# Pooled attention and two MoE layers: a different weight conversion, q transposed on TensorE, half of the k/v pooling in the DMA

## The chip, the cores and the metric

The kernel runs on one core of a Trainium2 chip. The metric is device time in microseconds (us), shorter is better. The engines are called PE (TensorE matmul), PEld (its weight loads), DVE (VectorE), ACT (ScalarE), POOL (GpSimd) and SP (SyncE, which here issues DMAs).

## What is computed

Three parts in float32, one after the other. Weights arrive as 64-bit floats.

```python
# q, k, v: (8 batches, 8 heads, 576, 64)
k_p = k.reshape(B, H, 72, 8, D).mean(axis=3)      # v_p likewise
scores = (1 / sqrt(D)) * q @ k_p.T
attn = exp(scores - max); attn /= attn.sum() + 1e-9
x = (attn @ v_p), as (4608 tokens, 512)
x = ((x @ w1) * (x @ w2)) @ w3 @ w_out            # d_ff 1024
xn = x / sqrt(mean(x * x) + 1e-6) * rms_g
out = (silu(xn @ w_gate) * (xn @ w_val)) @ w_out2 # d_ff 1536
```

## The kernel before, in words

**Numbers.** Every wide product runs as three float32r matmuls (`mm3`, L87 to L90): each operand is split into hi and lo (`split`, L83: ACT copies hi, DVE subtracts), and hi*hi, hi*lo and lo*hi accumulate in PSUM. (a*b) @ w3 @ w_out is computed as (a*b) @ (w3 @ w_out).

**Weights.** `Conv` (L96) turns 64-bit floats into float32. Step s0 loads 128 x 512 words of 64 bits into a tile raw. Step s1: ACT scales the low word (L115); DVE takes the sign out of the high word (L116) and masks the sign off its top 16 bits (L119); ACT subtracts 14336 from those 16 bits and clips at zero (L122, the rebias of the exponent). Step s2: DVE shifts the high word by 3 and ors the sign in (L125) and adds the low part (L133). Step s3 splits. `conv_steps` staggers the steps of successive jobs. There are 76 jobs: 24 for w3 and w_out and 16 for w1 and w2 early on, 12 for the second w_out and 24 for w_gate and w_val later. Tiles raw have 5 buffers for the first 24 jobs and 3 for the rest; the k/v loads share those 3.

**Stages.** Phase 0 forms w3 @ w_out (16 stages of four transposes and four float32 matmuls), with the attention of batch 0, the first half of w1 and w2 and the first products beside it. Phase 1 goes through nine blocks of 512 tokens. Per block there are eight steps m: two wide products (12 matmuls each; the second is multiplied into the first by DVE, L627, giving f, which is split into hh and hl), then the second product (12 matmuls) of the step before. Beside the products of block i runs the attention of batch i + 1. Phase 2 is the gated layer over nine blocks, without attention.

**Attention of a batch** (`att_steps`, L216). k and v are pooled from raw buffers by `pool_pair` (L197): two heads a load, 72 partitions, three halving adds on DVE (L205 twice, L209). kp is transposed on PE and copied to kT by ACT (L247, L248). q is transposed (`step_Q`, L250): for batches 0 and 1 on PE with ACT copies (L271, L276), for the others in 32 x 32 blocks on DVE (L265), 40 instructions a batch. Per tile of 128 rows, five a batch, and per half of the heads: score matmuls (L289), maximum on DVE (L301), its scaling (L302), four exponentials on ACT (L305). Then the normalization (`step_N`, L314): for batches 0 and 1 one DVE multiplication (L324), else eight ACT scalings (L322). Then the transposes to aT (`step_T`, L331), for batches from 2 on by DVE (L339, 54 a batch). `av_step` (L387) multiplies aT with vp and writes xh (ACT, L402) and xl (DVE, L403), the input of a block.

**What sets the order.** `Ticker` spreads these steps over a block's 24 slots, three a step m; `att_of(i)` (L630) lists them, and the block finishes them within 3 * 8 - 1 = 23 slots (L691). A scheduler then orders each engine's instructions; on the chip every engine runs its queue in that order, and an instruction that waits holds up those behind it. SP issues the DMAs in its own order too. PSUM has four buffers ps, used by products, scores, transposes and attention-value matmuls alike, and four for y. At a block's end `y_end` (L580) squares and copies y, sends it to DRAM and forms row sums; POOL computes their power -0.5 (L609).

Of the kernel before, what the change touches and what calls it, by code (L numbers as in the profile page):

```python
# [8 lines left out]
F32 = mybir.dt.float32  # L9
# [3 lines left out]
U16 = mybir.dt.uint16  # L13
# [8 lines left out]
def kernel(  # L22
# [15 lines left out]
    # Float32 products run as three float32r passes: every operand is split  # L38
    # exactly into hi (12 significant bits) + lo (the remaining 12), and
    # hi*hi + hi*lo + lo*hi accumulate in PSUM.  # L40
    # (a*b) @ w3 @ w_out is computed as (a*b) @ (w3 @ w_out).
# [50 lines left out]
    # float64 words -> float32 bits, round to nearest even.  The weights come in  # L92
    # as 64-bit words; the exponent is rebased (14336 = (1023 - 127) << 4, with
    # values below float32's range going to zero), the top 20 mantissa bits are
    # shifted into place and the next 32 bits are rounded to the last 3.
    class Conv:  # L96
# [11 lines left out]
        def s1(self):  # L108
# [3 lines left out]
            top = self.raw.bitcast(U16).rearrange("p (n w) -> p n w", w=4)[:, :, 3]  # L112
            if self.out is None:
# [3 lines left out]
                out=self.out, in0=self.hiw, scalar1=-(2**31), scalar2=None, op0=ALU.bitwise_and  # L117
            )
            nc.vector.tensor_scalar(  # L119
                out=top, in0=top, scalar1=0x7FFF, scalar2=None, op0=ALU.bitwise_and  # L120
            )
            nc.scalar.activation(top, top, AF.Relu, bias=nbias)  # L122

        def s2(self):
            nc.vector.scalar_tensor_tensor(  # L125
                out=self.out,
                in0=self.hiw,
                scalar=3,
                in1=self.out,
                op0=ALU.logical_shift_left,  # L130
                op1=ALU.bitwise_or,
            )
            nc.vector.tensor_tensor(out=self.out, in0=self.out, in1=self.low, op=ALU.add)  # L133
# [29 lines left out]
    nbias = const.tile([P, 1], F32, name="nbias")  # L163
    nc.vector.memset(nbias, -14336.0)
# [32 lines left out]
    def pool_pair(dst, src, b, p):  # L197
        r = raw_p.tile([P, 1024], I32, tag="raw", name="kv")[:SP].bitcast(F32)
        r = r.rearrange("s (h c) -> s h c", h=2)
        nc.sync.dma_start(  # L200
            out=r, in_=src[b, 2 * p : 2 * p + 2].rearrange("h (s l) d -> s h (l d)", l=POOL)
        )
        n = POOL * D // 2
        while n > D:
            nc.vector.tensor_tensor(  # L205
                out=r[:, :, :n], in0=r[:, :, :n], in1=r[:, :, n : 2 * n], op=ALU.add
            )
            n //= 2
        nc.vector.tensor_tensor(  # L209
            out=dst.rearrange("s (h d) -> s h d", d=D)[:, 2 * p : 2 * p + 2, :],  # L210
# [5 lines left out]
    def att_steps(b):  # L216
        q_t, qT_t, s_t, mx_t, den_t = {}, {}, {}, {}, {}
# [10 lines left out]
        def step_k0():  # L228
            st8["kp", b] = at_p.tile([SP, H * D], F32, tag="kp", name="kp")
            for p in range(2):  # L230
                pool_pair(st8["kp", b], k, b, p)

        def step_k1():
            load_q(0)
            for p in range(2, NP):
                pool_pair(st8["kp", b], k, b, p)
            load_q(1)

        def step_kT():
# [7 lines left out]
            nc.scalar.copy(kT[:D, :, :SP], pv[:D])  # L247
            nc.scalar.copy(kT[D:, :, SP:], pv[D:])  # L248

        def step_Q(g, hf):  # L250
# [8 lines left out]
            if b >= 2:  # L259
                src = qt.rearrange("s u (p c) -> s u p c", p=NP)  # L260
                for i in range(2 * hf, min(2 * hf + 2, n // 32)):
                    rows = slice(32 * i, 32 * i + 32)
                    for j in range(4):
                        cols = slice(32 * j, 32 * j + 32)
                        nc.vector.transpose(  # L265
                            qT[cols, :nu, :, rows], src[rows, :nu, :, cols]
                        )
            elif hf < nu:
# [14 lines left out]
        def step_S(t, hf):  # L283
# [17 lines left out]
            nc.vector.tensor_reduce(out=mx, in_=pv, axis=AX.X, op=ALU.max)  # L301
            nc.vector.tensor_scalar_mul(mx, mx, -ATT_SCALE)  # L302
            for j in range(4):
# [6 lines left out]
                    scale=ATT_SCALE,  # L310
# [3 lines left out]
        def step_N(t):  # L314
# [4 lines left out]
            if b >= 2:  # L319
                for h in range(H):  # L320
                    z = s_t[t][:n, h, :SP]
                    nc.scalar.activation(z, z, AF.Copy, scale=den[:n, h, :])  # L322
                return
# [29 lines left out]
        def step_v(ps_):  # L353
            if ps_[0] == 0:
                st8["vp", b] = at_p.tile([SP, H * D], F32, tag="vp", name="vp")
            for p in ps_:
                pool_pair(st8["vp", b], v, b, p)
# [24 lines left out]
        steps[5:5] = [lambda: step_v((0, 1))]  # L382
        steps[11:11] = [lambda: step_v((2, 3))]
# [255 lines left out]
    class Pipe:  # L639
        """The two wide products of m, then the second product of m - 1."""  # L640
# [49 lines left out]
    for i in range(1, NB - 2):  # L690
        pipe.run(i, range(KF1), ab, y_mm, Ticker(att_of(i), 3 * KF1 - 1))  # L691
        xt.pop(i)
# [150 lines left out]
```

## Time and profile before

| | |
|---|---|
| time, median of 3 runs | 1769.09 us (1768.5 to 1769.53) |
| span of the profiled execution, its own time | 1769.0 us |
| PE busy | 1691.3 us, 96% |
| DVE busy | 1011.3 us, 57% |
| ACT busy | 680.2 us, 38% |
| POOL busy | 11.4 us, 1% |
| DMA | 100.17 MB, mean 57 GB/s |

The span runs from the first to the last instruction of one profiled execution; nothing of that execution's time lies outside it that the profile shows. Busy is the union of an engine's instructions. Matmuls overlap in the pipeline and their ends are modelled, so PE's busy time says little of how close it is to its peak; the number of matmuls in a stretch says more. PEclk is the TensorE clock that was granted, 1.00 being 2.4 GHz and 0.50 being 1.2 GHz. A wait is put down to what came last by the profile.

### The profile page before, as it was taken

What the parts mean: (1) busy time and instruction counts of PE and PEld (TensorE: products, weight loads), DVE (VectorE), ACT (ScalarE), POOL (GpSimd) and SP (SyncE); (2) the same over time, 40 slices, a digit from 0 to 9 for tenths busy, and PEclk for the clock granted to TensorE, in tenths of its full rate; (3) what the DMA queues carried; (4) which work ended last, traced back from release to release, by engine and by line L of the source; (5) the groups of instructions that cost most, each with busy time, mean ns of one, the idle gap of its engine ahead of it and who ended that gap; (6) DMA issues with size and microseconds to landing.
All of it is one profiled execution on the core that took longest, in us unless ns stands there. A gap on an engine that the chain in (4) does not pass through costs nothing.

```text
span 1769.0 us, 19994 instructions
## 1 busy us (share of the span) xinstructions
PE 1691.3 (96%) x7418; PEld 1323.9 (75%) x7418; DVE 1011.3 (57%) x2060; ACT 680.2 (38%) x1706; POOL 11.4 (1%) x17
## 2 busy tenths in 40 slices
PE   6989998989898989899999999999999999999999
PEld 3557676767676767678777888888888888888887
DVE  8988898878797967664895232323223232323222
ACT  8977454535353535553783121212111111212111
POOL 0000000000000000000000000000000000000000
PEclk9999999989999989999999999999999999999999
DMA  7745213021212120231452000100000000000000
GB/s 238 200 126 138 75 37 86 20 78 27 79 26 73 32 70 1 72 96 45 133 149 67 31 24 24 30 25 30 23 8 24 30 24 24 19 24 7 24 1 24
DMA packets 84371, 100.17 MB, mean 57 GB/s; under 512 B 44201, under 2 KB 52393, under 8 KB 84274
## 3 DMA queue, kind: packets, MB, share of 16 engines
q1 hardware_dynamic: 84274, 98.90, 19.2%
q8 instruction: 58, 0.95, 0.2%
q14 instruction: 39, 0.32, 0.1%
HBM read 79.97 MB, written 18.91 MB: 56 GB/s over the span
## 4 chain that ended last, share of the span: by engine, by line
PE 64%; DVE 23%; ACT 8%; DMA 3%; issue 2%; SPq 0%; ACTq 0%; DVEq 0%
PE ps L88 14%; PE ps L89 14%; PE ps L90 13%; DVE aT L339 7%; PE y L88 7%; PE y L90 7%; PE y L89 7%; DVE qT L265 3%; ACT raw L122 3%; DVE hl L85 2%; PE ps L395 2%; DVE raw L119 1%; DVE f L627 1%; DVE kv L205 1%; ACT s L322 1%
## 5 line engine op out<-in xcount | busy, mean ns | idle before, releaser
L772 DVE TENSOR_TENSOR f<-ps,f 128x512 f32<-128x512 f32 x108 | 74.7, 691 | 370.1 <-ACT f L771 369.9
L84 ACT CAST hh<-f 128x512 fp32r<-128x512 f32 x185 | 114.7, 620 | 356.3 <-DVE f L775 269.3
L771 ACT ACTIVATE f<-ps 128x512 f32<-128x512 f32 x108 | 64.7, 599 | 384.2 <-PE ps L90 384.0
L85 DVE TENSOR_TENSOR hl<-f,hh 128x512 fp32r<-128x512 f32 x185 | 127.9, 692 | 85.3 <-ACT hh L84 83.6
L88 PE MATMUL y<-o2h,hh 128*128 128x512 f32 x432 | 170.8, 395 | 1.5 <-ACT hh L84 1.5
L90 PE MATMUL y<-o2h,hl 128*128 128x512 f32 x432 | 171.0, 396 | 0.0
L89 PE MATMUL y<-o2l,hh 128*128 128x512 f32 x432 | 170.6, 395 | 0.0
L90 PE MATMUL ps<-xnh,vl 128*128 128x512 f32 x432 | 168.2, 389 | 2.0 <-DVE vl L85 2.0
L89 PE MATMUL ps<-xnl,gh 128*128 128x512 f32 x432 | 169.0, 391 | 0.6 <-DVE xnl L738 0.5
L88 PE MATMUL ps<-xnh,gh 128*128 128x512 f32 x432 | 168.5, 390 | 0.6 <-ACT xnh L737 0.6
L88 PE MATMUL ps<-xnh,vh 128*128 128x512 f32 x432 | 168.6, 390 | 0.5 <-ACT vh L84 0.5
L90 PE MATMUL ps<-xnh,gl 128*128 128x512 f32 x432 | 168.5, 390 | 0.0
L89 PE MATMUL ps<-xnl,vh 128*128 128x512 f32 x432 | 168.3, 390 | 0.0
L339 DVE STREAM_TRANSPOSE aT<-s 32x256 f32<-32x256 f32 x324 | 140.9, 435 | 21.4 <-ACT s L322 15.7
L775 DVE TENSOR_TENSOR f<-ps,f 128x512 f32<-128x512 f32 x108 | 74.7, 691 | 131.2 <-PE ps L90 131.1
L88 PE MATMUL ps<-xh,w2h 128*128 128x512 f32 x288 | 122.3, 425 | 24.4 <-DVE xl L403 19.9
L305 ACT ACTIVATE s<-ps,mx 128x72 f32<-128x72 f32 (+1 forms) x320 | 98.0, 322 | 80.9 <-DVE mx L302 80.8
L88 PE MATMUL y<-hh,wph 128*128 128x512 f32 x288 | 118.6, 412 | 8.9 <-DVE wpl L85 4.5
L88 PE MATMUL ps<-xh,w1h 128*128 128x512 f32 x288 | 118.1, 410 | 2.6 <-ACT s L305 1.3
L122 ACT ACTIVATE raw<-raw,nbias 128x512 uint16<-128x512 uint16 x76 | 110.4, 1460 | 25.6 <-DVE raw L119 25.2
L89 PE MATMUL ps<-xl,w2h 128*128 128x512 f32 x288 | 118.6, 412 | 0.0
L90 PE MATMUL ps<-xh,w2l 128*128 128x512 f32 x288 | 117.9, 409 | 0.0
(110 smaller groups left out, 3061.6 us busy)
## 6 DMA issues: line engine op xcount, KB each, us to landing
raw<-in_moe_w_dram SPq DMA_DIRECT2D x32, 512.0 KB
raw<-in_moe_w_out_dram SPq DMA_DIRECT2D x20, 512.0 KB
kv<-in_k_dram SPq DMA_DIRECT2D x32, 288.0 KB
kv<-in_v_dram SPq DMA_DIRECT2D x32, 288.0 KB
ydram<-f SPq DMA_DIRECT2D x36, 256.0 KB
raw<-ydram SPq DMA_DIRECT2D x18, 512.0 KB
out_dram<-f SPq DMA_DIRECT2D x36, 256.0 KB
q<-in_q_dram SPq DMA_DIRECT2D x32, 256.0 KB
```

The source lines that it names most:

```text
L84: nc.scalar.copy(hi, src)
L85: nc.vector.tensor_tensor(out=lo, in0=src, in1=hi.bitcast(F32), op=ALU.subtract)
L88: nc.tensor.matmul(o, lh, rh, start=first, stop=False)
L89: nc.tensor.matmul(o, lh, rl, start=False, stop=False)
L90: nc.tensor.matmul(o, ll, rh, start=False, stop=last)
L122: nc.scalar.activation(top, top, AF.Relu, bias=nbias)
L265: nc.vector.transpose(qT[cols, :nu, :, rows], src[rows, :nu, :, cols])
L305: nc.scalar.activation(s_t[t][:n, h, :SP], pv[:, j, :], AF.Exp, bias=mx[:, j, :], scale=ATT_SCALE, accum_out=den_t[t][:n, h, :],)
L339: nc.vector.transpose(aT[32 * kb : 32 * kb + 32, :, s0 + 32 * i : s0 + 32 * i + 32], s_t[t][32 * i : 32 * i + 32, :, 32 * kb : 32 * kb + 32],)
L771: nc.scalar.activation(sg, ps, AF.Sigmoid)
L772: nc.vector.tensor_tensor(out=sg, in0=ps, in1=sg, op=ALU.mult)
L775: nc.vector.tensor_tensor(out=hf, in0=ps, in1=a0.pop((i, m)), op=ALU.mult)
```

## The change

1. Conversion: instead of the masking of 16-bit words and ACT's rebias, DVE multiplies the high word, read as a float32, by 2**-112 (which takes 896 off the exponent), and shifts the result by 3 (L117, L120 of the new kernel). The sign is ored into the low part. ACT keeps one operation a job, DVE four.
2. Pooling: a load takes four heads, but only the first four of each eight rows; a second DMA, issued by POOL, adds the other four rows onto them in place (`accum_op=ALU.add`). DVE then adds twice instead of three times, for half as many loads. Loads and sums are separate steps now: k's loads in step_k0, its sums in step_k1; v's loads after the fourth step, its sums seven steps later.
3. The score scale is applied in the copy to kT; the maximum is taken with its sign reversed, so its scaling (L302) goes.
4. q is transposed on PE, with ACT copies, for all batches; the normalization is the one DVE multiplication for all batches. The aT transposes stay as they are.
5. In blocks 1 to 6 the attention steps are spread over 3 * 8 - 4 = 20 slots.

```diff
@@ -109,25 +110,24 @@
             w2_ = self.raw.rearrange("p (n w) -> p n w", w=2)
             self.hiw, self.low = w2_[:, :, 1], w2_[:, :, 0]
             low_u = self.raw.bitcast(U32).rearrange("p (n w) -> p n w", w=2)[:, :, 0]
-            top = self.raw.bitcast(U16).rearrange("p (n w) -> p n w", w=4)[:, :, 3]
+            hi_f = self.raw.bitcast(F32).rearrange("p (n w) -> p n w", w=2)[:, :, 1]
             if self.out is None:
                 self.out = ftile(I32)
             nc.scalar.activation(self.low, low_u, AF.Copy, scale=2.0**-29)
             nc.vector.tensor_scalar(
-                out=self.out, in0=self.hiw, scalar1=-(2**31), scalar2=None, op0=ALU.bitwise_and
+                out=self.out.bitcast(F32), in0=hi_f, scalar1=2.0**-112, scalar2=None, op0=ALU.mult
             )
             nc.vector.tensor_scalar(
-                out=top, in0=top, scalar1=0x7FFF, scalar2=None, op0=ALU.bitwise_and
-            )
-            nc.scalar.activation(top, top, AF.Relu, bias=nbias)
+                out=self.out, in0=self.out, scalar1=3, scalar2=None, op0=ALU.logical_shift_left
+            )
         def s2(self):
             nc.vector.scalar_tensor_tensor(
-                out=self.out,
+                out=self.low,
                 in0=self.hiw,
-                scalar=3,
-                in1=self.out,
-                op0=ALU.logical_shift_left,
+                scalar=-(2**31),
+                in1=self.low,
+                op0=ALU.bitwise_and,
                 op1=ALU.bitwise_or,
             )
             nc.vector.tensor_tensor(out=self.out, in0=self.out, in1=self.low, op=ALU.add)
@@ -194,27 +192,28 @@
     pools[0] = x0_p
     st8 = {}
-    def pool_pair(dst, src, b, p):
+    def pool_four(src, b, g):
         r = raw_p.tile([P, 1024], I32, tag="raw", name="kv")[:SP].bitcast(F32)
-        r = r.rearrange("s (h c) -> s h c", h=2)
-        nc.sync.dma_start(
-            out=r, in_=src[b, 2 * p : 2 * p + 2].rearrange("h (s l) d -> s h (l d)", l=POOL)
+        r = r.rearrange("s (h c) -> s h c", h=4)
+        n = POOL * D // 2
+        w = src[b, 4 * g : 4 * g + 4].rearrange("h (s l) d -> s h (l d)", l=POOL)
+        nc.sync.dma_start(out=r, in_=w[:, :, :n])
+        nc.gpsimd.dma_start(out=r, in_=w[:, :, n:], accum_op=ALU.add)
+        return r
+    def pool_sum(dst, r, g):
+        nc.vector.tensor_tensor(
+            out=r[:, :, : 2 * D], in0=r[:, :, : 2 * D], in1=r[:, :, 2 * D :], op=ALU.add
         )
-        n = POOL * D // 2
-        while n > D:
-            nc.vector.tensor_tensor(
-                out=r[:, :, :n], in0=r[:, :, :n], in1=r[:, :, n : 2 * n], op=ALU.add
-            )
-            n //= 2
         nc.vector.tensor_tensor(
-            out=dst.rearrange("s (h d) -> s h d", d=D)[:, 2 * p : 2 * p + 2, :],
+            out=dst.rearrange("s (h d) -> s h d", d=D)[:, 4 * g : 4 * g + 4, :],
             in0=r[:, :, :D],
             in1=r[:, :, D : 2 * D],
             op=ALU.add,
         )
     def att_steps(b):
-        q_t, qT_t, s_t, mx_t, den_t = {}, {}, {}, {}, {}
+        q_t, qT_t, s_t, mx_t, den_t, kv_t = {}, {}, {}, {}, {}, {}
         def load_q(g):
             if 2 * g >= NTL:
@@ -226,14 +225,13 @@
                 )
         def step_k0():
-            st8["kp", b] = at_p.tile([SP, H * D], F32, tag="kp", name="kp")
-            for p in range(2):
-                pool_pair(st8["kp", b], k, b, p)
+            kv_t["k"] = [pool_four(k, b, g) for g in range(2)]
         def step_k1():
             load_q(0)
-            for p in range(2, NP):
-                pool_pair(st8["kp", b], k, b, p)
+            st8["kp", b] = at_p.tile([SP, H * D], F32, tag="kp", name="kp")
+            for g, r in enumerate(kv_t.pop("k")):
+                pool_sum(st8["kp", b], r, g)
             load_q(1)
         def step_kT():
@@ -244,8 +242,8 @@
                     ps[:, p * SP : (p + 1) * SP], kp[:, p * P : (p + 1) * P], ident[:SP, :SP]
                 )
             pv = ps[:, : NP * SP].rearrange("d (p s) -> d p s", p=NP)
-            nc.scalar.copy(kT[:D, :, :SP], pv[:D])
-            nc.scalar.copy(kT[D:, :, SP:], pv[D:])
+            nc.scalar.activation(kT[:D, :, :SP], pv[:D], AF.Copy, scale=ATT_SCALE)
+            nc.scalar.activation(kT[D:, :, SP:], pv[D:], AF.Copy, scale=ATT_SCALE)
         def step_Q(g, hf):
             if 2 * g >= NTL:
@@ -256,16 +254,7 @@
             if hf == 0:
                 qT_t[g] = at_p.tile([P, 2, NP, P], F32, tag="qT", name="qT", bufs=2)
             qT = qT_t[g]
-            if b >= 2:
-                src = qt.rearrange("s u (p c) -> s u p c", p=NP)
-                for i in range(2 * hf, min(2 * hf + 2, n // 32)):
-                    rows = slice(32 * i, 32 * i + 32)
-                    for j in range(4):
-                        cols = slice(32 * j, 32 * j + 32)
-                        nc.vector.transpose(
-                            qT[cols, :nu, :, rows], src[rows, :nu, :, cols]
-                        )
-            elif hf < nu:
+            if hf < nu:
                 ps = psum()
                 for p in range(NP):
                     nc.tensor.transpose(
@@ -298,8 +287,7 @@
                 mx_t[t] = at_p.tile([P, H, 1], F32, tag="mx", name="mx", bufs=2)
                 den_t[t] = at_p.tile([P, H, 1], F32, tag="den", name="den", bufs=2)
             mx = mx_t[t][:n, 4 * hf : 4 * hf + 4, :]
-            nc.vector.tensor_reduce(out=mx, in_=pv, axis=AX.X, op=ALU.max)
-            nc.vector.tensor_scalar_mul(mx, mx, -ATT_SCALE)
+            nc.vector.tensor_reduce(out=mx, in_=pv, axis=AX.X, op=ALU.max, negate=True)
             for j in range(4):
                 h = 4 * hf + j
                 nc.scalar.activation(
@@ -307,7 +295,6 @@
                     pv[:, j, :],
                     AF.Exp,
                     bias=mx[:, j, :],
-                    scale=ATT_SCALE,
                     accum_out=den_t[t][:n, h, :],
                 )
@@ -316,11 +303,6 @@
             den = den_t.pop(t)
             nc.vector.tensor_scalar_add(den[:n], den[:n], 1e-9)
             nc.vector.reciprocal(out=den[:n], in_=den[:n])
-            if b >= 2:
-                for h in range(H):
-                    z = s_t[t][:n, h, :SP]
-                    nc.scalar.activation(z, z, AF.Copy, scale=den[:n, h, :])
-                return
             nc.vector.tensor_tensor(
                 out=s_t[t][:n, :, :SP],
                 in0=s_t[t][:n, :, :SP],
@@ -350,11 +332,13 @@
             dst = aT[:SP, 4 * hf : 4 * hf + 4, s0 : s0 + n]
             nc.scalar.copy(dst, src)
-        def step_v(ps_):
-            if ps_[0] == 0:
-                st8["vp", b] = at_p.tile([SP, H * D], F32, tag="vp", name="vp")
-            for p in ps_:
-                pool_pair(st8["vp", b], v, b, p)
+        def load_v():
+            kv_t["v"] = [pool_four(v, b, g) for g in range(2)]
+        def step_v():
+            st8["vp", b] = at_p.tile([SP, H * D], F32, tag="vp", name="vp")
+            for g, r in enumerate(kv_t.pop("v")):
+                pool_sum(st8["vp", b], r, g)
         pre = [step_k0, step_k1]
         steps = [step_kT, lambda: step_Q(0, 0), lambda: step_Q(0, 1)]
@@ -379,8 +363,8 @@
                     step_T(t - 1, 1)
             steps += [a, bq, c, d, e]
-        steps[5:5] = [lambda: step_v((0, 1))]
-        steps[11:11] = [lambda: step_v((2, 3))]
+        steps[4:4] = [load_v]
+        steps[11:11] = [step_v]
         steps += [lambda: step_T(NTL - 1, 0), lambda: step_T(NTL - 1, 1)]
         return pre, steps
@@ -688,7 +672,7 @@
     xt.pop(0)
     for i in range(1, NB - 2):
-        pipe.run(i, range(KF1), ab, y_mm, Ticker(att_of(i), 3 * KF1 - 1))
+        pipe.run(i, range(KF1), ab, y_mm, Ticker(att_of(i), 3 * KF1 - 4))
         xt.pop(i)
     for st in att_of(NB - 2):
```

On DVE, at the end of block 1 before (xl_1721 belongs to block 2, of which 384 columns are the newly attended batch; xl_2478 is block 3's; f is a step's product, hl its low part):

```order
L403 SCALAR_TENSOR_TENSOR xl_1721<-ps,xh_1720 128x384
L265 STREAM_TRANSPOSE qT<-q 32x8x32 x9
L403 SCALAR_TENSOR_TENSOR xl_1721<-ps,xh_1720 128x384
L265 STREAM_TRANSPOSE qT<-q 32x8x32
L403 SCALAR_TENSOR_TENSOR xl_1721<-ps,xh_1720 128x384
L265 STREAM_TRANSPOSE qT<-q 32x8x32 x3
L627 TENSOR_TENSOR f<-ps,f 128x512
L403 SCALAR_TENSOR_TENSOR xl_1721<-ps,xh_1720 128x384
L85 TENSOR_TENSOR hl<-f,hh 128x512
L403 SCALAR_TENSOR_TENSOR xl_2478<-ps,xh_2477 128x192 x2
L627 TENSOR_TENSOR f<-ps,f 128x512
L403 SCALAR_TENSOR_TENSOR xl_2478<-ps,xh_2477 128x192
```

The same place now (xl_1609 is block 2's, xl_2291 block 3's, L611 is f, L84 hl):

```order
L387 SCALAR_TENSOR_TENSOR xl_1609<-ps,xh_1608 128x384 x2
L611 TENSOR_TENSOR f<-ps,f 128x512
L387 SCALAR_TENSOR_TENSOR xl_1609<-ps,xh_1608 128x384
L84 TENSOR_TENSOR hl<-f,hh 128x512
L387 SCALAR_TENSOR_TENSOR xl_1609<-ps,xh_1608 128x384
L611 TENSOR_TENSOR f<-ps,f 128x512
L84 TENSOR_TENSOR hl<-f,hh 128x512
L387 SCALAR_TENSOR_TENSOR xl_2291<-ps,xh_2290 128x192 x3
L611 TENSOR_TENSOR f<-ps,f 128x512
```

Block 2's xl moved ahead by one step m (there is an f and an hl between them and block 3's xl), and no qT transposes stand among them.

On DVE right behind that, now, around the start of the next block (vp and kp are the pooled v and k, L208 their last add, which frees a buffer kv; L205 is the first add of a freshly loaded kv; L574 and L577 are y_end's):

```order
L208 TENSOR_TENSOR vp<-kv 72x256
L387 SCALAR_TENSOR_TENSOR xl_2291<-ps,xh_2290 128x192
L208 TENSOR_TENSOR vp<-kv 72x256
L84 TENSOR_TENSOR hl<-f,hh 128x512
L208 TENSOR_TENSOR kp<-kv 72x256
L574 COPY f<-y 128x512
L577 TENSOR_TENSOR f<-f 128x512
L574 COPY f<-y 128x512
L577 TENSOR_TENSOR f<-f 128x512 x2
L205 TENSOR_TENSOR kv<-kv 72x4x128
L84 TENSOR_TENSOR hl<-f,hh 128x512
L208 TENSOR_TENSOR kp<-kv 72x256
```

The first add of the second k load comes nine instructions after the sum that frees a buffer for that load.

On POOL, now, over a block (L201 are the adding DMAs, L593 the power for ss):

```order
L201 DMA kv<-in_k_dram 72x4x256
L201 DMA kv<-in_v_dram 72x4x256 x2
L201 DMA kv<-in_k_dram 72x4x256
L593 TENSOR_TENSOR ss<-ss,mhalf 128x4
L201 DMA kv<-in_k_dram 72x4x256
```

POOL had only the nine L609 there before; four DMAs a batch have come in between them.

## Rows read from the trace of the kernel before

**Rows 1.** The page's first part: busy us, share of the span, xinstructions of each engine.
```profile
PE 1691.3 (96%) x7418; PEld 1323.9 (75%) x7418; DVE 1011.3 (57%) x2060; ACT 680.2 (38%) x1706; POOL 11.4 (1%) x17
```

**Rows 2.** Stages (us): length, busy us (xinstructions) of each engine, granted PEclk, DMA share, GB/s.
```profile
0.00:46.00 46.00, 31.73 (x88) 14.97 (x88) 37.70 (x75) 36.75 (x43) 1.11 (x8) 1.00 0.78 239
46.00:187.00 141.00, 129.44 (x600) 89.22 (x599) 123.73 (x277) 109.21 (x284) 0.00 (x0) 0.99 0.53 144
187.00:709.90 522.90, 486.92 (x2207) 372.17 (x2206) 429.72 (x1048) 245.41 (x938) 6.93 (x6) 0.95 0.19 51
709.90:950.00 240.10, 228.03 (x970) 179.97 (x970) 168.95 (x293) 141.14 (x200) 3.36 (x3) 0.98 0.34 101
950.00:1769.00 819.00, 815.18 (x3559) 667.54 (x3557) 251.16 (x371) 147.69 (x243) 0.00 (x0) 1.00 0.06 22
370.30:380.00 9.70, 9.70 (x48) 7.03 (x48) 2.85 (x6) 2.10 (x5) 0.00 (x0) 1.00 0.26 56
386.00:420.00 34.00, 34.00 (x163) 28.21 (x163) 29.41 (x77) 17.48 (x74) 1.16 (x1) 1.00 0.35 90
1100.00:1200.00 100.00, 100.00 (x438) 81.94 (x437) 31.74 (x47) 18.64 (x31) 0.00 (x0) 1.00 0.07 24
```

**Rows 3.** Groups on PE by shape: first 386 to 420 us, then 370.3 to 380 us.
```profile
L289 PE MATMUL ps<-kT,qT 128*128 128x144 f32 x28 | 4.6, 285 | 0.0
...
L395 PE MATMUL ps<-aT,vp 72*64 72x256 f32 x12 | 1.7, 396 | 0.0
```

**Rows 4.** Waits from 273.4 to 709.9 us: us in total, times, longest us.
```profile
PE ps L88 <- DVE xl L403: 17.1, 5, 3.7
...
PE ps L395 <- DVE f L627: 7.4, 5, 2.2
...
PE ps L88 <- ACT s L305: 5.4, 5, 1.9
```

**Rows 5.** The chain of waits through 355 to 372 us, its shares by line.
```profile
by line: DVE qT L265 22.0%; DVE aT L339 13.0%; PE ps L88 12.2%; PE ps L89 10.0%; PE ps L90 10.0%; PE ps L395 6.2%; issue 5.5%; PE y L88 5.3%; PE y L90 4.1%; DVE f L627 4.1%; DVE hl L85 4.1%; PE y L89 4.0%; DVE xl L403 3.0%
```

**Rows 6.** Groups on DVE in one block, 360 to 448.6 us: xcount | busy us, mean ns | idle before.
```profile
L339 DVE STREAM_TRANSPOSE aT<-s 32x256 f32<-32x256 f32 x54 | 23.5, 435 | 2.9 <-ACT s L322 1.9
L265 DVE STREAM_TRANSPOSE qT<-q 32x256 f32<-32x256 f32 (+1 forms) x40 | 16.4, 409 | 0.7
L205 DVE TENSOR_TENSOR kv<-kv 72x512 f32<-72x512 f32 (+1 forms) x16 | 8.6, 547 | 3.3 <-DMA kv<-in_k_dram 2.2 <-DMA kv<-in_v_dram 1.1
L85 DVE TENSOR_TENSOR hl<-f,hh 128x512 fp32r<-128x512 f32 x9 | 6.2, 689 | 0.9 <-ACT hh L84 0.8
...
L209 DVE TENSOR_TENSOR kp<-kv 72x128 f32<-72x128 f32 x4 | 1.1, 286 | 0.0
```

**Rows 7.** Groups by shape over the whole span.
```profile
L122 ACT ACTIVATE raw<-raw,nbias 128x512 uint16<-128x512 uint16 x76 | 110.4, 1460 | 25.6 <-DVE raw L119 25.2
...
L119 DVE TENSOR_SCALAR raw<-raw 128x512 uint16<-128x512 uint16 x76 | 56.5, 746 | 0.3
...
L133 DVE CUSTOM_DVE_ANT_0 f<-raw,f 128x1024 uint16<-128x1024 uint16 x68 | 47.5, 699 | 0.2
...
L116 DVE TENSOR_SCALAR f<-raw 128x512 int32<-128x512 int32 x68 | 28.6, 421 | 6.2 <-DMA raw<-in_moe_w_dram 4.5 <-DMA raw<-in_moe_w_out_dram 1.0 <-DMA raw<-in_moe_w_val_dram 0.7
...
L324 DVE TENSOR_TENSOR s<-s,den 128x576 f32<-128x576 f32 x8 | 6.0, 748 | 0.0
...
L271 PE MATMUL ps<-ident,q 128*128 128x128 f32 x32 | 4.9, 274 | 0.0
```

**Rows 8.** The whole chain in order of time: start us, us, what.
```profile
386.81 5.50 DMA kv<-in_k_dram
...
570.25 3.20 DMA kv<-in_k_dram
```

More of the change, by code (lines that the diff above doesn't have):

```diff
@@ L12 @@
 U32 = mybir.dt.uint32
-U16 = mybir.dt.uint16
 AF = mybir.ActivationFunctionType
@@ L162 @@
     nc.vector.memset(mhalf, -0.5)
-    nbias = const.tile([P, 1], F32, name="nbias")
-    nc.vector.memset(nbias, -14336.0)
     ydram = dram_p.tile([NB, KD, P, TB], F32, name="ydram")
```

## The prediction

> **What bounds the kernel now.** I read the page first, then the busy time by stage, then inside one block, and last the chain of waits. On the page TensorE (PE) is busy 96% of the span, VectorE (DVE) 57%, ScalarE (ACT) 38% [rows 1]. The stages show what that mean hides: from 950 us to the end PE is busy 815 of 819 us at the full clock, the 2.4 GHz level, VectorE 251, and the change touches nothing there; before 950 VectorE is busy 70 to 88% and ACT 47 to 80% of each stage [rows 2]. Everything is decided before 950.
>
> Blocks 1 to 6 of phase 1 (187 to 709.9 us, one batch of attention beside each block's products) take 522.9/6 = 87.15 us each. What would PE alone need? Between 1100 and 1200 us 438 wide matmuls take 100 us, 0.228 us each; from 386 to 420 us there are 163, 28 of them score matmuls, so (34 - 135 x 0.228)/28 = 0.114 us a score matmul; from 370.3 to 380 us 48, 12 of them attention-value matmuls of 256 columns, so (9.7 - 36 x 0.228)/12 = 0.123 us [rows 2, 3]. A block has 288 wide ones (65.8), 40 score (4.6), 32 attention-value of 288 columns on average (32 x 0.123 x 288/256 = 4.4), four small transposes and two rms matmuls (about 1): 75.7 us. **So 11.4 us of each block are lost.** The waits say where: in the five blocks from 273.4 to 709.9 us PE stood 17.1 us for VectorE's xl and 7.4 us for its product f, once a block each, at the border between two blocks, and 5.4 us for ACT's exponentials in mid-block [rows 4]. That is 30/5 = 6.0 us idle a block. The granted clock of the stage is 0.95 [rows 2]; 0.05 x 87 is 4.4 us more, a tenth of the time at the 1.2 GHz level. Together 10.4, close to 11.4.
>
> What makes the border late? The chain through 355 to 372 us is VectorE first: 22.0% qT transposes (L265), 13.0% aT transposes (L339), 3.0% xl [rows 5]. PE doesn't wait for a long operation but for a queue: qT transposes stand ahead of the xl that free its PSUM buffers.
>
> **The change, part by part.** *In blocks 1 to 6.* VectorE loses per block 40 qT transposes (16.4 us). Of the k/v sums, 8.6 us for the two halvings, 1.1 for kp's last step and as much for vp's, 10.8 in all, there remain four adds of 512 and four of 256 elements, by the same mean of 547 ns 4.4 us [rows 6]. It gains five normalizations at 748 ns, 3.7 us, which leave ACT [rows 7]. Net 16.4 + 6.4 - 3.7 = 19.1 us less, of 429.7/6 = 71.6 [rows 2]: 52.5 us in a block of some 80. (The ten small scalings of mx go too; I don't price them.) PE gains 20 q transposes; between a score matmul's 0.114 us and 4.9/32 = 0.153 us [rows 7] that is 2.3 to 3.1, and I take 2.5, nearer to the first because a row's busy time counts overlapping ends. New floor 78.2 us. The scale of the scores moves into kT's copy, the same two instructions: nothing.
>
> The 20 slots matter as much. In the order rows the xl of a block's own batch stood directly ahead of the next batch's; now a whole product f with its hl stands between, so they are asked for one step m, 36 wide matmuls or 8.2 us, earlier. The border wait was 24.5/5 = 4.9 us, behind 16.4 us of work that will not be in the queue. I count the border as gone, its half clock with it. The price of the 20 slots is density: scores, exponentials and most aT transposes of a batch now lie within about four steps m, where PE needs 4 x 8.2 us and some 6 of attention, 38 us. Outside it VectorE has thirteen operations at 0.69 (four f, four hl, five of y_end), eight xl at less than that and the last ten aT transposes at 0.435 [rows 6]: about 9 + 5 + 4.4 = 18, so 34 us of its 52.5 lie inside. Nearly full; so I keep the mid-block wait (5.4/5 us, its clock about as much again) and add a half for late kv sums: residual 3.0. **81.2 us a block, gain 5.95 x 6 = 35.7 us.**
>
> *The accumulating DMA* is the unknown; no row shows one. A buffer that VectorE's vp sum frees is filled by a plain DMA, then POOL waits for that landing and issues the accumulate, and VectorE's next kv sum waits for the second landing, in its fixed place. The plain half costs 3.2 to 5.5 us by the chain's pieces for kv loads of the same 288 KB [rows 8]. From below I price the second half at the same, 6.4 together; as the upper end I keep four times the slower piece, 22 us, since a read-add-write could be far slower; and I take 11, twice the slower piece. Its cover: the sum stands behind y_end's five operations, which need another 12 matmuls (2.7 us) and cost 5 x 0.69 themselves, about 7 us in all with the hl ahead. So VectorE may stand some 4 us a block, at its start, where the next m's f isn't due for a further 4. POOL's only other work, the pow for ss, stands ahead of the k load in the order rows.
>
> The Trainium skill (DMA: Bandwidth & Descriptors, "Anatomy of one DMA — SWDGE (gpsimd) path") gives a DMA from GpSimd about 2.0 us plus its bytes at 436 GB/s; by that the accumulate would take an estimated 2.7 us, no kv sum would wait, and with a residual of 2.5 the time would be 1707. No row here shows such a DMA, so the sum stays with the bounds above.
>
> *The conversion* (76 of them). ACT loses L122, 1460 ns each, 110.4 us in all. On VectorE a masking of 746 ns (L119) gives way to a shift; its nearest row is the other one-source operation on 128x512 words, 421 ns (L116), which I take, with 421 and 746 as bounds: up to 0.325 us less each, 2.24 instead of 2.56 with the two unchanged ones of 0.70 [rows 7]. From 0 to 46 us the first 16 conversions set the pace, 46/16 = 2.9 us each, though VectorE is busy only 37.7 us; L122 stands in each chain between two of its operations. Without it VectorE paces; its durations overlap a little (37.7 us now for 16 x 2.56 = 41), so about 2.0 us. That could save 13 us; but 512 KB every 2.0 us is 262 GB/s, and 239 GB/s take 0.78 of the DMA engines [rows 2], so I take 9. From 46 to 187 us PE is idle 11.6 us and the clock costs 0.01 x 141 = 1.4, with ACT at 77%: 8 us. From 709.9 to 950 us, 36 conversions beside the products, 12.1 us are idle and 0.02 x 240 = 4.8 go with the clock; ACT drops by 52.6 of 141 us, VectorE by up to 11.7: a third, 6 us [rows 2, 7].
>
> **Sum:** 9 + 8 + 35.7 + 6 = 58.7 us. The profiled span is 1769.0 us [rows 1], 0.1 below the median of the three runs, 1769.09; so 1710 us.
>
> **Rivals.**
> (a) VectorE stays the bound in its dense stretch. For it: 34 of 38 us, and an order that can't step aside. Blocks then gain 2.5 us instead of 6: 15 + 23 = 38 us, 1731; if the other stages give only half too, 1743.
> (b) All that VectorE and ACT caused goes. Residual 0.5 a block: 8.45 x 6 = 51 us; 24 ahead of 187 us, 10 at the later conversions: 85 us, 1684. Against it: the dense stretch.
> (c) Slower. One mechanism: the accumulate lands so late that VectorE's queue stands in every block, f and hl behind the kv sum, PE behind those. Decisive point: the cover is 7 us, f's slack 4; to eat 58.7/6 = 9.8 us a block the two transfers must take over 7 + 4 + 9.8 = 21 us. At 25 us it costs 4 x 6 = 24: 1793. Against it: twice 5.5 is 11. For it: four such chains a block go through one queue, and no row shows one.
> (d) The first stages give nothing. VectorE's one-source operations hold up POOL's issue: a conversion has two, 2 x 0.421 of each 2.0 us [rows 7], so a transfer of 5.5 us stretches to 5.5 x 2.0/1.16 = 9.5, 4 us more in the sums of five tensors ahead of 187 us: 20 us, more than the 17 expected there; 58.7 - 20 = 38.7, 1730. Against it: those sums stand behind other conversions, so part is covered. This is what the Trainium skill (SBUF — State Buffer, "Who interferes with whom") states as a rule: a VectorE operation in a two-port mode locks GpSimd out, which can then not write its DMA's descriptors. By that rule blocks 1 to 6, which have no conversions, keep their gain.
> (e) The change doesn't do what it says: xl are not ready earlier, since aT ends when it did, and q's 15 us on PE (2.5 x 6) and the denser mid-block eat the rest: 1769. The order rows speak against it.
>
> **Chances.** Forecast 0.50 (its own range 1698 to 1724), (a) 0.15, (b) 0.19, (c) 0.07, (d) 0.05, (e) 0.04. A measurement of this kernel can tell about 0.2%, 3.5 us. Faster by more 0.89, within 0.04, slower 0.07. The range goes from 1690, inside (b), to 1744, just past the far end of (a); left out are (c), (e) and half of (b), about 0.2.
>
> **What would show it.** Right: PE's waits for xl and f at the borders gone, the granted clock of blocks 1 to 6 from 0.95 to 0.98 or more, a block near 81 us, the first 16 conversions done about 37 us in instead of 46, and 950-to-end unchanged in length. Wrong: VectorE waiting for kv DMAs over 4 us a block; PE's wait for ACT's exponentials grown past 3 us a block; a shift at 746 ns; q transposes over 0.15 us each. The size is wrong if PE's idle time ahead of 187 us doesn't shrink by about 17 us.

## The result: 1737.8 us, half of the gain that was forecast

The changed kernel takes 1737.76 us (median of four runs, 1734.58 to 1739.47) against 1769.31 us before: ratio 0.9824, interval 0.9809 to 0.984, a gain of 31.5 us. The forecast was 1710 us, a gain of 58.7, with a range to 1744: the direction is right and the time lies in the range, but the range reached that far for another reason, rival (a); the gain was put nearly twice too high.

The page's first part of the changed kernel, beside [rows 1]:

```profile
PE 1687.5 (97%) x7538; PEld 1332.8 (77%) x7538; DVE 869.6 (50%) x1641; ACT 537.6 (31%) x1420; POOL 52.0 (3%) x49
```

VectorE and ACT lost some 142 us of work each, PE gained 120 instructions (the q transposes). To see where the gain is, both traces are cut at the same two marks, the first w1 product of block 1 and that of block 7 (199.8 and 724.8 us before; 197.5 and 701.8 us now; the prediction's stages, cut some 13 us earlier, are the same work but for the overlap at the edges). The spans of the two traces, 1769.0 and 1735.2 us, are 33.8 us apart, 2.3 more than the medians; the gains of the stages add up to that.

| us | before | now | gain | forecast |
|---|---|---|---|---|
| up to block 1 | 199.8 | 197.5 | 2.3 | 17 |
| blocks 1 to 6 | 525.0 | 504.3 | 20.7 | 35.7 |
| from block 7 on | 1044.2 | 1033.4 | 10.8 | 6 |

The stages of the changed kernel, columns as in [rows 2]:

```profile
0.00:46.00 46.00, 36.15 (x100) 16.85 (x100) 37.16 (x81) 19.69 (x31) 3.91 (x10) 1.00 0.97 284
46.00:197.50 151.50, 135.29 (x626) 94.18 (x625) 99.72 (x207) 82.14 (x272) 13.26 (x11) 0.95 0.56 127
197.50:701.80 504.30, 488.24 (x2335) 381.04 (x2333) 330.42 (x709) 196.17 (x721) 30.56 (x25) 0.99 0.23 51
```

In blocks 1 to 6 VectorE fell to 330 of 504 us, and PE is still idle for 16 of them. From 46 us to block 1 the granted clock is 0.95; between 46 and 199.8 us of the kernel before it was 0.97. Something new stands in the way in both stages. The waits of blocks 1 to 6, beside [rows 4]:

```profile
DVE kv L205 <- DMA kv<-in_k_dram: 21.4, 5, 4.5
...
PE ps L584 <- DVE hl L84: 14.5, 5, 3.7
...
DVE kv L205 <- DMA kv<-in_v_dram: 12.2, 8, 2.5
```

The old border waits for xl and f are gone but for 0.6 us on f. In their place PE waits once at each of five borders for hl of the row sums (L584, the second of the two rms matmuls of `y_end`). The chain of waits at the start of block 1 says why hl is late (start us, us, what):

```profile
209.99 5.59 DMA kv<-in_k_dram
...
215.61 0.06 DVE kv L205
...
216.22 0.69 DVE hl L84
...
216.95 0.39 PE ps L584
217.35 0.43 PE ps L89
...
220.33 0.43 PE ps L87
220.76 0.24 PE ps L88
```

and VectorE's timeline shows who stood in front of whom:

```profile
210.61 0.69 DVE L577 TENSOR_TENSOR f<-f 128x512 f32<-128x512 f32 x1 [0.73 <-ACT f L569]
215.61 0.69 DVE L205 TENSOR_TENSOR kv<-kv 72x512 f32<-72x512 f32 x1 [4.31 <-DMA kv<-in_k_dram]
216.22 0.68 DVE L84 TENSOR_TENSOR hl<-f,hh 128x512 fp32r<-128x512 f32 x1
```

and ACT's, when the other input of hl was there:

```profile
212.29 0.63 ACT L83 CAST hh<-f 128x512 fp32r<-128x512 f32 x1
```

VectorE has nothing to do from 211.3 us on, hl could be made at 212.9, but the first add of a k load stands ahead of it and waits 4.31 us for the adding DMA. PE waits behind hl, and then eight matmuls run at 0.43 us, at the 1.2 GHz level, where 0.23 is the rate of the 2.4 GHz level. The clock falls like that at four of the five borders (217, 302, 470 and 555 us); at the one at 386 us the matmuls behind a wait of 2.78 us run at 0.23. In all that is 14.5 us of waiting and about 4 x 8 x 0.2 = 6.4 us of half clock. The kp that the late sum makes is read by PE's next four kp transposes (L241), and these stand far behind in the same chain:

```profile
289.00 0.41 PE ps L241 x4
```

The sum that holds the border at 215 us isn't needed for another 70.

Ahead of block 1 it is the same DMA in other clothes (VectorE's and PE's waits, 0 to 197.5 us):

```profile
DVE kv L205 <- DMA kv<-in_v_dram: 24.8, 6, 6.7
...
PE ps L328 <- DVE s L306: 7.1, 2, 3.7
...
DVE kv L205 <- DMA kv<-in_k_dram: 6.2, 4, 3.2
...
PE ps L278 <- ACT s L293: 3.3, 1, 3.3
```

31.0 us of VectorE waiting for kv where the kernel before had 1.7; the normalizations (L306) and maxima behind it are late, and PE's transposes and scores with them, as in this stretch of the chain:

```profile
163.23 10.09 DMA kv<-in_v_dram
173.34 0.69 DVE kv L205
...
175.13 0.68 DVE s L306
175.86 1.58 PE ps L328 x8
177.44 0.43 PE ps L87
```

This DMA is the sixth of v, so it belongs to batch 2, whose attention runs beside block 1.

### The profile page after: what moved, and what is told of

It reads as the page before. It is cut to its first block, busy times and chain, and to the rows that moved or that the text cites. A ratio compares the mean times of both kernels' runs of the same rounds, so it can differ in the third digit from the quotient of the medians.

```text
span 1735.2 us, 19499 instructions
## 1 busy us (share of the span) xinstructions
PE 1687.5 (97%) x7538; PEld 1332.8 (77%) x7538; DVE 869.6 (50%) x1641; ACT 537.6 (31%) x1420; POOL 52.0 (3%) x49
## 4 chain that ended last, share of the span: by engine, by line
PE 77%; DVE 7%; DMA 5%; ACT 2%; issue 1%; POOL 0%; SPq 0%; DVEq 0%; POOLq 0%; ACTq 0%
PE ps L87 17%; PE ps L89 16%; PE ps L88 16%; PE y L87 8%; PE y L89 8%; PE y L88 8%; DVE aT L321 3%; DMA kv<-in_v_dram 2%; DMA kv<-in_k_dram 2%; PE ps L379 2%; PE ps L278 1%; DVE f L611 0%; DVE s L306 0%; DVE hl L84 0%; ACT f L569 0%
## 5 line engine op out<-in xcount | busy, mean ns | idle before, releaser
L84 DVE TENSOR_TENSOR hl<-f,hh 128x512 fp32r<-128x512 f32 x185 | 127.9, 691 | 89.0 <-ACT hh L83 87.6
L88 PE MATMUL y<-hl,wph 128*128 128x512 f32 x288 | 113.7, 395 | 0.0
```

The source lines that it names most:

```text
L84: nc.vector.tensor_tensor(out=lo, in0=src, in1=hi.bitcast(F32), op=ALU.subtract)
L88: nc.tensor.matmul(o, lh, rl, start=False, stop=False)
```

## The experiments

Ratios are to runs of the kernel before taken beside each; the last three columns are the marks above, from the one traced execution of each run (that of pool_only took 8 us more than its median).

| run | median us | ratio (interval) | up to block 1 | a block, 1 to 6 | from block 7 |
|---|---|---|---|---|---|
| changed kernel | 1737.8 | 0.9824 (0.9809 to 0.984) | 197.5 | 84.0 | 1033.4 |
| no_acc | 1692.0 | 0.9567 (0.9553 to 0.9581) | 172.9 | 80.3 | 1033.9 |
| plain_pool | 1696.2 | 0.9588 (0.9572 to 0.9604) | 178.0 | 80.7 | 1033.0 |
| pool_sums | 1714.5 | 0.9694 (0.9678 to 0.9711) | 192.9 | 81.5 | 1033.8 |
| second_pool | 1738.2 | 0.9825 (0.9806 to 0.9844) | 198.5 | 84.3 | 1033.3 |
| second_sp | 1696.2 | 0.9594 (0.9577 to 0.9611) | 175.9 | 80.4 | 1033.8 |
| acc_in_order | 1707.2 | 0.9648 (0.9634 to 0.9662) | 192.1 | 80.4 | 1033.9 |
| mixed | 1696.5 | 0.958 (0.9567 to 0.9593) | 180.9 | 80.4 | 1034.0 |
| plain_23 | 1696.0 | 0.9594 (0.9579 to 0.9608) | 178.8 | 80.7 | 1032.6 |
| before + conversion (conv_only) | 1740.8 | 0.9842 (0.9828 to 0.9857) | 186.6 | 86.9 | 1030.6 |
| before + q and normalization (q_on_pe) | 1727.8 | 0.9768 (0.9754 to 0.9781) | 194.3 | 81.3 | 1043.8 |
| before + 20 slots (slots20_only) | 1767.9 | 0.9994 (0.9985 to 1.0004) | 199.4 | 87.1 | 1044.8 |
| before + pooling (pool_only) | 1807.3 | 1.0215 (1.0192 to 1.0238) | 223.2 | 90.5 | 1047.6 |

### Is it the adding DMA? (no_acc, plain_pool)

`no_acc` leaves out one line:

```diff
         nc.sync.dma_start(out=r, in_=w[:, :, :n])
-        nc.gpsimd.dma_start(out=r, in_=w[:, :, n:], accum_op=ALU.add)
```

> The changed kernel with POOL's adding DMA left out: half of each pooling window is missing from kp and vp, the rest is as it was. Theory A (the landing of the second DMA holds VectorE's queue, and with it hl of the row sums at each block border and the first v and k sums): VectorE's waits for kv, 64.6 us in the changed kernel, fall below 15; PE's waits for hl at the borders, 14.5 us, fall below 4; the time falls by the 14.5 us, some 7 us of half clock behind them and 7 to 10 us ahead of 187 us: 1706 us (1700 to 1716). Theory B (what is left of the loss is the dense middle of a block, and the kv waits only fill time in which VectorE had nothing due): 1730 us or more, with another wait in the place of the one for hl.

Measured 1692.0 us, 46 less than the changed kernel and below theory A's range (1700 to 1716): more hung on this DMA than its border waits. Of PE's waits in blocks 1 to 6, 0.5 us are left.

`plain_pool` puts `pool_pair` and its steps of the kernel before into the changed kernel (`step_k0`, `step_k1`, `step_v`), with the loads and sums where they stood.

> The changed kernel with the pooling of the kernel before: one DMA for two heads, three adds on VectorE, no adding DMA. Theory A: the border waits go as without the adding DMA, and VectorE's extra 6.4 us a block cost at most 1 us a block: 1714 us (1706 to 1724). Theory B (VectorE's dense stretch decides, and the halved sums were worth their 6.4 us a block): blocks 1 to 6 grow by 1 to 3 us each: 1742 to 1755 us.

Measured 1696.2 us, below theory A's range too: it leaves nothing out and beats both kernels. Its blocks 1 to 6 and the waits in them:

```profile
178.00:661.90 483.90, 482.09 (x2334) 377.25 (x2332) 352.18 (x794) 196.19 (x721) 7.56 (x6) 1.00 0.20 55
```
```profile
DVE kv L203 <- DMA kv<-in_k_dram: 3.7, 3, 1.6
...
PE ps L581 <- ACT hh L83: 1.3, 2, 0.8
...
PE ps L87 <- DVE f L609: 0.2, 1, 0.2
```

VectorE works 22 us more there than in the changed kernel (352 against 330 us), PE idles 1.8 us instead of 16, and the clock is 1.00. Theory B, the dense middle of a block, falls: more VectorE work in the same slots, and no wait of PE on it worth naming.

### Sums on POOL (pool_sums)

```diff
     def pool_sum(dst, r, g):
-        nc.vector.tensor_tensor(
+        nc.gpsimd.tensor_tensor(
...
-        nc.vector.tensor_tensor(
+        nc.gpsimd.tensor_tensor(
```

> The changed kernel with the kv sums on POOL, behind its own adding DMAs; VectorE keeps none of them. Theory A: VectorE's queue no longer waits for kv, PE's border waits for hl fall below 4 us, time 1706 us (1698 to 1718), a little below the run without the adding DMA since VectorE is also 4.4 us a block lighter. Theory B: 1730 us or more. A third way: POOL's sums are so slow, or so much in VectorE's way, that kT comes late: PE waits for kp or kT, over 1738 us.

Measured 1714.5 us. VectorE no longer waits, and blocks 1 to 6 come to 81.5 us, so the border is freed in this way too. But the gain ahead of block 1 is mostly missing (192.9 us). An add that takes VectorE 686 ns (mean, changed kernel) takes POOL 1287 (median):

```profile
L205 POOL TENSOR_TENSOR kv<-kv x32: 1272/1287/2281, 31.0 to 546.6; 72x512 f32<-72x512 f32 x32
```

### Adding, or where the second half comes from? (second_pool, second_sp)

The second DMA as a copy over the first, issued by POOL in second_pool; second_sp has `nc.sync` in the place of `nc.gpsimd`:

```diff
-        nc.gpsimd.dma_start(out=r, in_=w[:, :, n:], accum_op=ALU.add)
+        nc.gpsimd.dma_start(out=r, in_=w[:, :, n:])
```

> The changed kernel with POOL's second DMA as a plain copy over the first one instead of an addition onto it: half of each pooling window is missing from the sums; VectorE's order and the chain of two landings are as in the changed kernel. Theory C1 (the price is the length of the chain: a landing, then POOL's issue and the start of its transfer, and not the adding): 1732 to 1740 us, VectorE's waits for kv again about 65 us. Theory C2 (the read-add-write in the transfer is what takes long): a landing 3 us or more earlier, waits for kv under 35 us, 1700 to 1715 us.

Measured 1738.2 us, the changed kernel's time: the adding itself is not the price. VectorE's order at the border is the same, row for row, and so are the two waits that belong to it. VectorE's waits for v in blocks 1 to 6 fell from 12.2 to 1.2 us and a block takes 84.3 us against 84.0, so those cost next to nothing. The last line is POOL's second DMA (whole run), 6.6 us in the median with the addition:

```profile
DVE kv L205 <- DMA kv<-in_k_dram: 23.5, 5, 5.2
...
PE ps L584 <- DVE hl L84: 16.4, 5, 3.8
```
```profile
DMA to landing us min/median/max: 3.5/6.3/8.5
```

> The same, a plain copy of the second half over the first, but issued by SP: two landings in a row, without POOL (half of each pooling window is missing from the sums). Its order has the late sum two rows behind hl. Theory C1 with POOL's share of the chain as the larger one: kv waits under 25 us, 1695 to 1708 us. If any two landings in a row are too long for where the sums stand: 1720 us or more.

Measured 1696.2 us, the lower end of theory C1. This run doesn't separate two things, though: the chain has no POOL in it, and the scheduler, which takes another landing time for it, set the late sum three rows behind hl, after a maximum and an f. Which of the two frees the border, the next edit shows.

### The same DMAs, the sums later (acc_in_order, mixed)

All adding DMAs stay; a sum may not be placed ahead of the last low part that stands before it in the program (`split` notes its latest subtraction as `last["lo"]`):

```diff
+        with tc.issue_after(last["lo"].ins):
             nc.vector.tensor_tensor(
                 out=r[:, :, : 2 * D], in0=r[:, :, : 2 * D], in1=r[:, :, 2 * D :], op=ALU.add
```

VectorE's order near the end of block 1 then has both k sums of the next batch together, just ahead of block 2's first xl, and none at the border:

```
L86 TENSOR_TENSOR hl<-f,hh 128x512
L210 TENSOR_TENSOR kv<-kv 72x4x128 x2
L213 TENSOR_TENSOR kp<-kv 72x256 x2
L392 SCALAR_TENSOR_TENSOR xl_1609<-ps,xh_1608 128x384 x2
```

> The changed kernel, adding DMAs and all, with one edit: a kv sum may no longer be placed on VectorE ahead of the hl (or other low part) that stands before it in the program. In the changed kernel the sums of a batch stand up to a block ahead of their use, right where their transfers land; here both k sums come about five steps m after their loads, just ahead of the block's own xl. Theory D1 (the transfer's length costs nothing by itself; it costs because VectorE's fixed order stands in front of it with hl behind): waits for kv under 10 us, PE's border waits for hl gone, 1690 us (1684 to 1698), as without the adding DMA or better. Theory D2 (the POOL-issued transfers cost wherever the sums stand, by what they do to other transfers or to VectorE): 1710 us or more. Theory D3: sums so late delay kT at the next block's start: PE waits for kp or kT, 1700 to 1720 us.

Measured 1707.2 us, 31 less than the changed kernel, though above D1's 1698 and, as a number, in the range of D3. Blocks 1 to 6 take 80.4 us each, as without the adding DMA (80.3); their waits:

```profile
PE ps L588 <- ACT hh L85: 0.5, 2, 0.3
...
PE ps L91 <- DVE f L616: 0.4, 1, 0.4
...
PE ps L384 <- DVE xl L392: 0.3, 1, 0.3
```
```profile
DMA to landing us min/median/max: 5.1/5.6/9.1
```

The transfers are 1 us shorter in the median (the last line, whole run), and nobody waits for them, nor PE for kp or kT. So in the blocks the price was the place of the sum on VectorE (D1), not the transfer. D2 and D3 fall there. Ahead of block 1 the edit gives 5.4 of the 19.5 us between the changed kernel and plain_pool; VectorE's waits for kv there fall from 31.0 to 8.5 us, and yet most of the early loss is left, so it is not all VectorE standing for a sum. `mixed` uses plain pooling for batches 0 and 1 and this for the others.

> Plain pooling for batches 0 and 1, the adding DMA with sums held in program order for batches 2 to 7; everything else as in the changed kernel. Stage by stage: up to the first second product of block 1 as with plain pooling (191.8 us), blocks 1 to 6 as with the sums in order (480.1 us): the sum is 1695 us (1690 to 1700), the same as plain pooling. If the adding DMAs of batch 2, which load ahead of block 1, disturb the early conversions all the same, 1700 to 1708 us.

Measured 1696.5 us, blocks as forecast: 80.4 us each by the marks of the table. Up to block 1 it takes 180.9 us, against 192.1 in acc_in_order and 178.0 with plain pooling throughout: 11.2 of the 19.5 us belong to the adding pooling of the first two batches, 5.4 to the place of the sums of whatever batch. Whether the 11.2 are the length of the transfers, the raw buffers that they hold longer beside the conversions, or POOL's queue was not tried apart. Two landings in a row do not cost it by themselves: second_sp has them, though copies without POOL and in another order, and is at 175.9 us. The 1696.5 us are also plain_pool's time: what the adding DMA saves VectorE is worth nothing once VectorE isn't the bound.

### The parts alone (conv_only, q_on_pe, slots20_only, pool_only, plain_23)

Each is the kernel before with one part of the diff as it stands above; plain_23 is plain_pool with `3 * KF1 - 1` slots.

> The kernel before with the new weight conversion and nothing else. The prediction's terms for it, 9 us to 46 us, 8 to 187 us and 6 behind 709.9 us, give 1746 us; if they were eaten in the changed kernel by the kv waits ahead of 187 us (31.0 us on VectorE, against 1.7 in the kernel before), they show here in full: 1742 to 1750. If the terms were too large by themselves (DMA at 0.97 of its engines in the first 46 us of the changed kernel), about 4 us ahead of 187 us and 10 behind 709.9 us come: 1753 to 1758.

Measured 1740.8 us: 26.7 us, close to the 23 of the forecast. In its profiled execution (span 1738.7, 30.3 below that of the kernel before) 13.2 us come ahead of block 1, 13.6 behind the mark of block 7, 3.5 in between.

> The kernel before with q transposed on PE and the one-multiplication normalization for all batches, and nothing else: old conversion, old pooling, 23 slots. The prediction's theory (the qT transposes in VectorE's queue make the border late): blocks 1 to 6 go from 87.2 to about 81 us each, the rest stays: 1730 us (1724 to 1740). The rival (several of the causes must go together): the border's waits shrink by half or less, 1745 to 1765 us.

Measured 1727.8 us: 41.1 us; in its trace blocks 1 to 6 gain 37.2, at 81.3 us a block. The transposition and the normalization were not tried apart, and the second may have a share: in the kernel before VectorE's aT transposes waited 15.7 us in these blocks for ACT's scalings (L322). PE's waits for xl and f are down to 0.3 us:

```profile
PE ps L88 <- ACT s L296: 2.8, 5, 0.9
PE ps L280 <- ACT s L296: 0.4, 1, 0.4
PE ps L88 <- DVE xl L389: 0.3, 1, 0.3
```

> The kernel before with 20 slots and nothing else. If the border's wait comes from the slots: up to 4.9 us a block less, 1745 to 1755 us. If it comes from VectorE's queue (qT transposes ahead of xl): the transposes only get denser, the waits for xl and for the exponentials stay or grow: 1764 to 1775 us.

Measured 0.9994, no difference. The border's wait stays (19.4 us on xl, L395 <- L403), and exponentials are waited for more.

> The kernel with the plain pooling (1696.2 us) with the attention steps spread over 23 slots, as in the kernel before. The prediction gives the 20 slots about half of the border's 4.9 us: PE's waits for xl or f at the borders come back, 1704 to 1716 us. The rival: without the qT transposes VectorE's queue is short enough that xl is on time either way: 1694 to 1699 us.

Measured 1696.0 us against 1696.2: the slots are worth nothing with short queues either.

> The kernel before with the new pooling (adding DMAs, sums apart) and nothing else. If the fixed place of the sums on VectorE is the price, it is paid here too, less what VectorE saves: slower than before, 1775 to 1800 us. The rival: in the kernel before VectorE reaches the sums so late, behind the qT transposes, that the landings are hidden and its 6.4 us a block are a gain: 1750 to 1766 us.

Measured 1807.3 us, 37.5 slower, beyond the first range (1775 to 1800). VectorE waits for kv 40.2 us in blocks 1 to 6 and 26.6 ahead of them, and the old border waits stay.

The four parts alone add up to -26.7 - 41.1 - 0.8 + 37.5 = -31.1 us; the whole change measures -31.5. That is closer than the runs can tell, since the intervals reach some 2 to 4 us either way; the scaling of the scores had no run of its own, and the adding DMA with its sums costs 39.9 us in the changed kernel (the gain of plain_pool, 71.4, less 31.5) and 37.5 alone. Three parts gave 68.6 us, one took 37.5 back.

## Why the prediction came out as it did

**What bounds the kernel** was right. The waits of [rows 4] and the qT share of [rows 5] named the queue ahead of xl, and taking the qT transposes out of it, together with the normalization, frees the border without any other part. The forecast for a block was 81.2 us; q_on_pe has 81.3, plain_pool 80.7. Rival (a) asked for a VectorE that stays the bound in mid-block; in blocks 1 to 6 of q_on_pe, plain_pool and acc_in_order PE waits under 1 us for VectorE in all.

**The 20 slots** were wrong as a reason: "The 20 slots matter as much". Both runs on them show nothing. That xl is asked for a step earlier was read from the order rows, but an xl that waits behind no queue is on time either way, and one behind a queue of transposes moves with the queue.

**The conversion** was right in sum, 26.7 us alone against 23, and in its prices: the shift took 420 ns where 421 was taken.

```profile
L120 DVE TENSOR_SCALAR f<-f 128x512 int32<-128x512 int32 x68 | 28.4, 420 | 0.3
```

The early part was put a little too large (17; alone it gives 13.2): the first 16 conversions end at 38.8 us in conv_only and at 38.5 in the changed kernel, against 46.0, and 37 was forecast. What keeps the rest is not shown; the DMA engines are at 0.87 in the first 46 us of conv_only and at 0.97 in the changed kernel. The late part was put too small (6; it gives 13.6): I took "a third" of 17 us of idle time and half clock, and nearly all of it goes (PE idles 1.55 us from 701.8 to 940 us, and the clock is 1.00).

```profile
701.80:940.00 238.20, 236.65 (x1037) 193.31 (x1036) 157.42 (x285) 95.52 (x160) 4.30 (x3) 1.00 0.34 104
```

**The accumulating DMA** is the step that failed. Its size was well bounded: 11 us for both transfers was taken; at the border of block 1 the second took 5.59 us, in the median 6.6 (below), on top of a first of 3.2 to 5.5 [rows 8]. Even VectorE's wait was right: "VectorE may stand some 4 us a block, at its start"; it stood 21.4/5 = 4.3 us for the k load. With the waits for v it is (21.4 + 12.2)/6 = 5.6 us a block, over the 4 that the prediction names as a sign of being wrong. What failed is the rest of that sentence, "where the next m's f isn't due for a further 4". The instruction right behind the sum in the order rows is not f but an hl; I passed over it and didn't ask whose it is. It is the row sums', PE's next rms matmul needs it, and it has no slack. So 4.3 us on VectorE became 14.5/5 = 2.9 us on PE and 6.4/5 = 1.3 of half clock, against the half microsecond a block that the residual held. Ahead of 187 us the forecast priced no kv wait at all, outside rival (d): there the loss was as large (19.5 us between the changed kernel and plain_pool, 20.4 in blocks 1 to 6), and PE's idle time up to block 1 shrank only from 28.5 to 26.1 us, where 17 us less was the forecast.

That the time still lay in the range is in part luck, two errors of opposite sign. Without its half microsecond a block for late sums the forecast's gain was 61.7 us; without the adding DMA, in plain_pool, it is 71.4, between the forecast and rival (b). The other parts were put 10 us too small, the adding DMA 37 too small, at 3 us against 71.4 - 31.5 = 39.9.

Rival (c) had the mechanism, VectorE's queue standing for a late accumulate with PE behind it, and got its deciding point wrong for the same reason: not 21 us for both transfers but about 10 are enough, since f's slack doesn't count. Its sign was offset only by the other parts: alone, this part is slower. Of rival (d), the total came within 8 us and the place is in part right, but its cause doesn't show: POOL's issue is hardly drawn out among the conversions: 1.18 us at the least, 1.39 to 1.41 for three of the first four, and the longest, 1.46 us, at 463 us, where no conversion runs. The longest landing of 10.1 us, too, is at 163 us, behind the last early conversion (147.8 us).

```profile
L201 POOL DMA_DIRECT2D kv<-in_k_dram x16: 1183/1183/1413, 21.7 to 547.4; - x16
L201 POOL DMA_DIRECT2D kv<-in_v_dram x16: 1183/1183/1462, 54.1 to 559.4; - x16
...
DMA to landing us min/median/max: 4.9/6.6/10.1
```

The Trainium skill's rule for a DMA from GpSimd (DMA: Bandwidth & Descriptors, "Anatomy of one DMA — SWDGE (gpsimd) path"), which gave an estimated 2.7 us, does not agree with this trace: 4.9 us is the shortest, 6.6 the median of 32.

Why did the sum stand there at all? Not because anybody needed it: kp is read 70 us later. The order is fixed before the run; a sum without an ordering edge seems to be put where its load was taken to have landed (second_sp, whose second half comes from SP, has it elsewhere), and VectorE follows that order. acc_in_order, with the same transfers and another place, shows that the place was the price in the blocks. Ahead of block 1 that is shown for 5.4 of the 19.5 us; the cause of the rest stays open.

## What to carry to other kernels

When a change lengthens a transfer, don't ask whether somebody needs its result soon; ask what stands behind the first instruction that waits for it, on that engine, and who waits for that, with the owner of each hl or copy named. An operation far ahead of its use is harmless on an idle engine only if its input has landed; holding it back by one ordering edge bought 3.6 us a block here. And test parts alone: one of the four parts tested so took back more than half of what the others gave.

## What was not expected of the hardware

A second DMA from POOL that only copies (6.3 us in the median) took about as long to land as one that adds (6.6), although POOL's own part falls from 1183 to 712 ns. The shortest landings differ more, 3.5 against 4.9 us:

```profile
L201 POOL DMA_DIRECT2D kv<-in_v_dram x16: 712/712/715, 56.4 to 560.0; - x16
```

Where half clock came with one of PE's waits at the border it cost over half as much again as the wait: eight matmuls at 0.43 us instead of 0.23. The length of the wait alone doesn't decide it: the clock fell at the wait of 2.15 us (555 us) and not at the one of 2.78 us (386 us). And four parts whose waits looked entangled added up to about the whole.
